# New masks for the last three attention units, a place of its own for the second block's output, and sums inverted in two steps

## The chip, the cores and the metric

The kernel runs on one core of a Trainium2 chip. The metric is the device time of one execution in microseconds (us); the figure for the kernel before is the median of three runs. A profile is one more execution, recorded by the hardware profiler. PE is TensorE (matmul), PEld its weight load, DVE is VectorE, ACT is ScalarE, POOL is GpSimd, SP is SyncE, whose queue issues nearly all DMAs here. All five take their instructions strictly in the order in which the kernel wrote them.

## The reference

A transformer block for 2048 tokens of width 512: attention with 32 heads of 16 in a sliding window of 256, then a SwiGLU feed-forward part of width 1792; both with a modulated layer norm ahead and a gate behind.

```python
mod = (silu(c) @ w_mod).reshape(1, 6, 1, -1)
sa, ca, ga, sb, cb, gb = ...
h = layernorm(x) * (1 + ca) + sa
q, k, v = ...                                  # h @ wqkv, 32 heads of 16
scores = einsum("bhqd,bhkd->bhqk", q, k) * 16 ** -0.5
mask = (i - j >= 0) & (i - j < 256)
o = softmax(where(mask, scores, -1e9)) @ v
x = x + ga * (o @ wo)
h = layernorm(x) * (1 + cb) + sb
out = x + gb * ((silu(h @ w1) * (h @ w3)) @ w2)
```

All of it is float32. Products of weights and activations are made from a high and a low part (float32r), three matmuls for one.

## The kernel before, in words

**Attention.** The 2048 tokens are four blocks b of 512 (`NB`), the 32 heads eight groups g of four (`NQ`); a unit u = 4g + b is one group on one block, 32 units. Three stages run beside each other on different units. `unit_a` projects q and k (L375), ScalarE and GpSimd split them (L381 to L393), and SP puts them into the tile `ring` (L399). `unit_b` makes scores once (L430), takes their maxima on VectorE (L437), turns the maxima (L452) and stores them as more rows of `ring` (L461). `unit_c` makes the scores again, transposed (L681), masks them, takes the exponential, multiplies with the values into `po` (L657), copies `po` (L746) and stores it to DRAM, `o_dr[b]` (L749). The store holds 16 rows of output a head and one row with the sum of its exponentials. Unit 28 to 31 are the last group on the four blocks: after unit 28 the first block is complete in DRAM, after unit 31 the last.

The window's two triangular masks have four forms, chosen per pair of score tiles by a string of eight letters, `MODE` for units 0 to 28 and `MODL` for the last `NL` = 3 units: D adds the mask on VectorE (L689) and ScalarE takes the exponential (L693); E adds it by a second matmul (L684), then L693; P copies the masked squares aside (L716, L718), GpSimd masks them (L726), ScalarE takes their exponential (L730); C merges the two half-empty squares into one (VectorE, L699), takes the exponential of two squares instead of three (L702), and GpSimd cuts the result apart (L709). Where fewer than three squares are left, C becomes D.

**Handover.** Each attention step has a written time in units; those before `TS` = 229.9 are emitted in that order. From there a planner, `Sched.deal`, places all the rest: a list scheduler with an engine's earliest free time, a key for each operation (the smallest key that is ready goes first), a model of DMA transfers and of TensorE's clock, and limits on PSUM banks (`CAPS`). The attention steps left over are `fixed`: they come at their written times (scaled by `KEY` = 1.715 us), the other operations in between. What is emitted is a fixed order for each engine; the keys come from the dictionary `K`.

The other operations: `load_wo` loads the gated output weights (L935) and splits them (L892 on ScalarE, L894 on GpSimd). `load_x1` loads x, 16 tiles (L942). For each block, `o_sums` loads the sums of 32 heads (L952), inverts them (L955) and stores them (L956); `o_part` loads, for each of four parts of eight heads, the output (L971) and its inverses spread over 16 rows (L966), multiplies (VectorE, L982) and splits into a high part (ScalarE, L975) and a low part (VectorE, L978). The loads go to four pairs of staging tiles, (qkr, qk0), (qk1, qk2), (wq00, wq10) and (wq01, wq11), the same for every block; the parts go to the tiles `o0` and `o1`, also the same for every block. `o_proj` multiplies with wo (L998, 48 matmuls a block), adds to x (L1005) and takes the statistics of the second layer norm (L901).

**FFN.** When attention has ended, its memory is closed and `fp_open` makes the FFN's tiles. `load_w` loads the first weights (L1058) and splits them. `ln2(0)` normalizes blocks 0 and 1 (L1109), turns them (L1123), modulates (L1127) and makes the operands (L1140, L1146, L1148); `ffn(half, p)` makes seven products (L1185) twice, gates them (L1208 to L1239), splits (L1255, L1258), and adds the down product (L1276) to x (L1281). Half 0 is blocks 0 and 1, half 1 blocks 2 and 3, with seven steps p each.

Of the kernel before, what the change touches and what calls it, by code (L numbers as in the profile page):

```python
# [8 lines left out]
F32 = mybir.dt.float32  # L9
# [24 lines left out]
MODL = 'DEEPDPDP'  # L34
# [19 lines left out]
CAPS = dict(up=4, dn=2)  # L54
# [6 lines left out]
def dve(n):  # L61
    return 0.067 + 0.00104 * n
# [34 lines left out]
class Sched:  # L97
# [35 lines left out]
    def deal(self):  # L133
# [17 lines left out]
        while left:  # L151
# [21 lines left out]
            if fixed and (best is None or fixed[0][0] <= best[0]):  # L173
                t, fn, e, occ = fixed.pop(0)
# [52 lines left out]

KINDS = dict(scores=("PE", 0.2), top=("DVE", 0.5), parts=("DVE", 0.4), turn=("PE", 0.11), cut=("ACT", 0.16),
# [5 lines left out]
K = dict(wo=0.404, x1=0.976, xb=10.248, opre=-0.989, op=-1.383, o=11.225, l2=2.47, f=35.44,  # L234
         fl=4.282, w=-0.051, dn=0.047, ds=0.032, l3=-43.931)
@with_exitstack
def block_kernel(ctx: ExitStack, tc: tile.TileContext, x, wqk, wv, wo, w13, w2, c, wmod, out):
# [623 lines left out]
    end = (last[-1][0] - TS) * KEY + 1.0  # L861
    fixed = [((t - TS) * KEY, fn, *KINDS[kind]) for t, _, fn, kind in last]
    names = [("st", STB)] * 3 + [("mx", MXB)] * 3 + [("pj", 1)]
    free = [end - 1.0] * 3 + [(8 * (NU - 3) + X["ob"] + 8 + X["tl"] + X["mr"][1] - TS) * KEY + 0.4] * 3 + [0.0]
# [56 lines left out]
    def turn_over():  # L921
# [6 lines left out]
    sch.op("NIL", turn_over, 0.0, 0.0, [], [("x1", t) for t in range(NT)] + [  # L928
        (w, p, k) for w in ("wo", "o") for p in range(2) for k in range(KC)])

    def x1(t):
        return z["x1"][:, t]
# [11 lines left out]
    def o_sums(b, key):  # L944

        v = {}
        src = [("o_dr", b, g) for g in range(NQ)]
        lt = "mT"

        def load():  # L950
            v["lt"] = a1.tile([P, P], F32, name="mT", bufs=2)
            nc.sync.dma_start(v["lt"], o_dr[b].rearrange("(h r) t -> h r t", r=32)[:, DH].rearrange(  # L952
                "h (s t) -> h s t", t=P))
        dma(load, key, src, [lt], 64)
        sch.op("DVE", lambda: nc.vector.reciprocal(v["lt"], v["lt"]), 0.9, key, [lt], [lt])  # L955
        dma(lambda: nc.sync.dma_start(r_dr[b].rearrange("h (s t) -> h s t", t=P), v["lt"]), key, [lt],  # L956
            [("r_dr", b)], 64)

    def o_part(b, k, key):

        v = {}
        on, rn = (("qkr", "qk0"), ("qk1", "qk2"), ("wq00", "wq10"), ("wq01", "wq11"))[k]
# [11 lines left out]
        def hi():  # L974
            nc.scalar.activation(z["o"][0][:, k], v["ot"], AF.Copy)  # L975

        def lo():
            nc.vector.tensor_tensor(out=z["o"][1][:, k], in0=v["ot"],  # L978
                                    in1=z["o"][0][:, k].bitcast(F32), op=ALU.subtract)
        dma(load, key, [("o_dr", b, 2 * k), ("o_dr", b, 2 * k + 1)], [on], 256, occ=0.65, more=1.3)  # L980
        dma(spread, key, [("r_dr", b)], [rn], 256, occ=0.67, more=0.7)
        sch.op("DVE", lambda: nc.vector.tensor_mul(v["ot"], v["ot"], v["rt"]), dve(512) + 0.1, key + 4,  # L982
               [on, rn], [on])
        sch.op("ACT", hi, act(512) + 0.1, key + 4, [on], [("o", 0, k)])
        sch.op("DVE", lo, dve(512) + 0.1, key + 4, [on, ("o", 0, k)], [("o", 1, k)])

    def o_proj(b, key):
# [4 lines left out]
        for i in range(4):  # L992
            bk = Bank("dn")
            t = 4 * b + i
            for k in range(KC):
                def go(i=i, k=k, bk=bk):
                    for n, (h, w) in enumerate(PARTS):
                        nc.tensor.matmul(ps(bk), z["o"][h][:, k, i * P:(i + 1) * P],  # L998
                                         z["wo"][w][:, k], start=(k == 0 and n == 0),
                                         stop=(k == KC - 1 and n == 2))  # L1000
                sch.op("PE", go, 3 * MM[512], key + 2.7 * i + 0.6 * k,
                       [y for kk in (range(KC) if k == 0 else (k,)) for y in
                        (("o", 0, kk), ("o", 1, kk), ("wo", 0, kk), ("wo", 1, kk))], [bk])
            kk = key + 2.7 * (i + 1)
# [392 lines left out]
```

## Time and profile before

| | |
|---|---|
| time, median of 3 runs | 1088.39 us (1086.97 to 1089.33) |
| profiled execution | 1088.08 us, span 1086.3 us |
| busy, share of the span | PE 92%, PEld 66%, DVE 68%, ACT 50%, POOL 51% |
| mean granted clock of TensorE | 0.962 |
| DMA | 131.67 MB, mean 121 GB/s |
| last stores of attention (L749), units 27 to 31 | issued at 505.68, 521.81, 539.46, 556.98, 570.34 us |
| first matmul of the projection, of the FFN | 552.98 us, 623.15 us |

The profile gives times from the start of the span. The granted clock is the share of full speed that TensorE was allowed; a busy TensorE at 0.5 does half the work. "A <- B" reads: A waited for B. SPq is the queue of SP.

### The profile page before, as it was taken

The page shows a single profiled execution, that of the slowest core. Times are in us where ns is not written, and L with a number is a line of the kernel's source. Part 1 is how long each engine was busy: PE and PEld are TensorE (multiplying, and loading weights), DVE is VectorE, ACT ScalarE, POOL GpSimd, SP SyncE. Part 2 cuts the span into 40 slices and gives each one's busy share as a digit, 9 for nine tenths or more (in the row PEclk, how much of TensorE's full clock was granted, in tenths as well). Part 3 has the DMA queues.
Part 4 walks back from the last instruction along what each step waited for, and adds up shares of the span by engine and source line. Part 5 has one row for each costly group of instructions (what it writes and reads, how often), then busy time and mean ns, then how long its engine had stood idle before and what let it go on. Part 6 is the DMA issues. An engine that isn't in the chain of part 4 may idle for free.

```text
span 1086.3 us, 17117 instructions
## 1 busy us (share of the span) xinstructions
PE 1004.3 (92%) x5420; PEld 721.3 (66%) x5420; DVE 738.3 (68%) x1907; ACT 545.2 (50%) x1229; POOL 558.5 (51%) x705
## 2 busy tenths in 40 slices
PE   5999999999999999899796999999998799999998
PEld 3677665566555656565454778888876588878786
DVE  7685677676767676667457975666666866666755
ACT  2435667667766766667553353333344444333322
POOL 7523555566665656564213466876764454353411
PEclk9999999999999999999678899999999899999999
DMA  7522555545454554545556244544432132212102
GB/s 280 175 50 50 147 119 128 128 110 130 115 157 115 133 111 127 127 117 133 166 180 185 78 165 160 176 143 151 147 125 88 50 115 87 88 57 84 54 20 77
DMA packets 74429, 131.67 MB, mean 121 GB/s; under 512 B 8546, under 2 KB 21346, under 8 KB 74212
## 3 DMA queue, kind: packets, MB, share of 16 engines
q1 hardware_dynamic: 73620, 129.54, 42.1%
q10 hardware_dynamic: 720, 1.05, 0.3%
q8 instruction: 43, 0.70, 0.3%
q14 instruction: 46, 0.38, 0.1%
HBM read 79.96 MB, written 30.41 MB: 102 GB/s over the span
## 4 chain that ended last, share of the span: by engine, by line
PE 53%; DVE 16%; DMA 13%; POOL 9%; issue 4%; ACT 3%; SPq 1%; POOLq 0%; ACTq 0%; DVEq 0%
PE mx L1185 9%; DMA ring<-qk 8%; PE st L1185 7%; PE st L1276 6%; POOL qk L393 5%; PE mx L1276 5%; PE mx L430 5%; PE pj L375 4%; PE po L657 4%; PE st L681 3%; PE st L595 3%; PE pj L1185 3%; DVE qk L1258 3%; POOL pt L709 2%; DVE g L1212 2%
## 5 line engine op out<-in xcount | busy, mean ns | idle before, releaser
L437 DVE CUSTOM_DVE_ANT_0 junk<-mx,mskq 128x384 bf16<-128x384 f32 (+2 forms) x512 | 267.6, 529 | 96.1 <-PE mx L430 93.0
L430 PE MATMUL mx<-ring 96*128 96x384 f32 (+2 forms) x512 | 179.4, 363 | 32.1 <-DMA ring<-qk 23.3
L681 PE MATMUL st<-ring 100*128 100x384 f32 (+2 forms) x512 | 162.5, 363 | 5.7 <-DMA ring<-mT 2.7
L894 POOL TENSOR_TENSOR w<-w,w 128x512 fp32r<-128x512 f32 (+2 forms) x60 | 109.1, 1838 | 106.5 <-ACT w L892 106.5
L430 PEld LDWEIGHTS mx<-ring 96*128 96x128 f32 x512 | 97.0, 194 | 94.4 <-DVE mt L437 40.9
L375 PE MATMUL pj<-hT,wq 128*128 128x512 f32 x384 | 156.6, 423 | 1.2 <-DVE hT L295 1.2
L709 POOL TENSOR_SCALAR_AFFINE_SELECT pt<-pt 128x256 f32<-128x256 f32 x204 | 81.8, 406 | 71.0 <-ACT pt L702 63.8
L681 PEld LDWEIGHTS st<-ring 100*128 100x128 f32 x512 | 101.1, 201 | 20.8 <-issue 5.1
L657 PE MATMUL po<-pt,vS 128*17 128x384 f32 (+2 forms) x1408 | 113.1, 406 | 0.0
L393 POOL TENSOR_TENSOR qk<-qkr,qk 128x512 fp32r<-128x512 f32 x64 | 82.2, 1285 | 40.1 <-ACT qkr L381 37.6
L693 ACT ACTIVATE pt<-st 128x384 f32<-128x384 f32 (+2 forms) x174 | 79.3, 460 | 46.1 <-PE st L684 32.1
L702 ACT ACTIVATE pt<-st 128x256 f32<-128x256 f32 x204 | 77.8, 396 | 46.8 <-DVE st L699 45.9
L375 PEld LDWEIGHTS pj<-hT,wq 128*128 128x128 f32 x384 | 73.4, 193 | 26.6 <-issue 18.5
L699 DVE COPY_PREDICATED st<-later,st 128x128 f32<-128x128 uint8 x204 | 59.8, 293 | 38.9 <-PE st L681 38.8
L1216 DVE TENSOR_TENSOR t<-st,t 128x512 f32<-128x512 f32 x62 | 42.3, 686 | 58.5 <-PE st L1185 50.5
L1185 PE MATMUL st<-b,w 128*128 128x512 f32 x300 | 74.8, 391 | 1.7 <-ACT b L1146 1.1
L1185 PE MATMUL mx<-b,w 128*128 128x512 f32 x276 | 69.4, 391 | 2.8 <-DVE b L1148 2.5
L1228 POOL TENSOR_TENSOR t<-t,t 128x512 f32<-128x512 f32 x28 | 36.8, 1315 | 68.1 <-DVE t L1216 68.0
L726 POOL TENSOR_SCALAR_AFFINE_SELECT sm<-sm 128x256 f32<-128x256 f32 x125 | 48.1, 407 | 41.9 <-ACT sm L716 39.1
L1185 PEld LDWEIGHTS st<-b,w 128*128 128x128 f32 x300 | 56.2, 188 | 14.6 <-ACT b L1146 1.5
L1185 PEld LDWEIGHTS mx<-b,w 128*128 128x128 f32 x276 | 51.7, 188 | 14.5 <-DVE b L1148 2.9
L892 ACT ACTIVATE w<-w 128x512 fp32r<-128x512 f32 (+2 forms) x60 | 46.2, 793 | 29.0 <-DMA w<-wsum 21.8
(190 smaller groups left out, 2021.2 us busy)
## 6 DMA issues: line engine op xcount, KB each, us to landing
ring<-qk SPq DMA_DIRECT2D x192, 128.0 KB
o_dr<-os SPq DMA_DIRECT2D x32, 256.0 KB
w<-wsum SPq DMA_DIRECT2D x16, 512.0 KB
w<-w2g SPq DMA_DIRECT2D x14, 512.0 KB
jb<-in_w SPq DMA_DIRECT2D x24, 256.0 KB
w<-wraw SPq DMA_DIRECT2D x16, 384.0 KB
wraw<-in_w SPq DMA_DIRECT2D x7, 768.0 KB
vS<-in_wmod SPq DMA_DIRECT2D x20, 256.0 KB
```

Source lines behind the costliest of these rows:

```text
L375: nc.tensor.matmul(v["ps"], WQ[g][w][:, n // 3], hTp(i, n // 3, b * BT, BT), start=(n == 0), stop=(n == 3 * KC - 1))
L393: nc.gpsimd.tensor_tensor(out=v[n], in0=v["raw"], in1=v[1].bitcast(F32), op=ALU.subtract)
L430: nc.tensor.matmul(v[i][:, :n], queries(NS, a, gq, 1), keys(NS, hh, a, k0, gq + 1 - k0), start=True, stop=True)
L437: nc.vector.tensor_tensor_reduce(out=junk[:, :n], in0=v[i][:, :n], in1=mskq[:, 3 * P - n:], scale=1.0, scalar=-3e38, op0=ALU.add, op1=ALU. ...
L657: nc.tensor.matmul(po[32 * i:32 * i + DH + 1, qb * P:(qb + nq) * P], vS[:, kb, 4 * g + i], pts[i // 2][:, i % 2, c0:c0 + nq], start=first, ...
L681: nc.tensor.matmul(ps[:, :nq], keys(NM, hh, a, kb, 1), queries(NM, a, kb, nq), start=True, stop=not plus)
L693: nc.scalar.activation(held[u, j, a][:, hh, :nq], v[j, a, hh][:, :nq], AF.Exp, scale=SCALE)
L702: nc.scalar.activation(held[u, j, a][:, hh, :2], v[j, a, hh][:, :2], AF.Exp, scale=SCALE)
L709: nc.gpsimd.affine_select(out=pt[:, :, 2 * m], in_=pt[:, :, 0], **w)
L894: sch.op("POOL", lambda: nc.gpsimd.tensor_tensor(out=lo(), in0=src(), in1=hi().bitcast(F32), op=ALU.subtract), 0.06 + 0.0024 * n, key, [kr ...
L1185: nc.tensor.matmul(ps(bk), WT[s, n][w][:, col], BB[t, k][r], start=start and c == 0, stop=stop and c == 5, skip_group_check=True)
L1276: nc.tensor.matmul(ps(bk), tiles[hk + (h,)][:, i * P:(i + 1) * P], W2[y][:, f], start=(m == 0), stop=(m == 5))
```

## The change

Five things change. (1) `MODL` becomes `CECECECE`: in units 29 to 31, of each two pairs of score tiles one merges and one adds its masks by matmul. (2) The sums of a block's first 24 heads are loaded, inverted and stored by a call of their own, which needs only groups 0 to 5; a second call does the last eight heads. A tile of the projection may begin when `n` parts (2, 3, 2, 3 for the four blocks) are there. For each part a table says whether VectorE or GpSimd multiplies and subtracts. (3) Block 1's parts go to a tile of their own, which lies where the second half of x is loaded later; that half is loaded after block 1's projection. (4) The planner's times for the attention steps are shortened towards the end (`TW`), and operations with negative keys may go ahead of an attention step on the same engine. (5) Nearly all keys of the handover and the spacing of the FFN's keys are new, and down products and projections may hold five PSUM banks instead of two.

```diff
-MODL = 'DEEPDPDP'
+MODL = 'CECECECE'
...
-CAPS = dict(up=4, dn=2)
+CAPS = dict(up=4, dn=5)
...
             if fixed and (best is None or fixed[0][0] <= best[0]):
+                t, e = max(free[fixed[0][2]], fixed[0][0]), fixed[0][2]
+                first = [o for key, _, o in ready[e] if key < 0 and o.est <= t and all(
+                    b.i is not None for b in o.bank)]
+                if first:
+                    best = max(free[e], first[0].est), first[0]
+                    fixed.insert(0, None)
...
+def us(t):
+    return KEY * (min(t, TW[0]) - TS + TW[2] * max(0.0, min(t, TW[1]) - TW[0]) + TW[3] * max(0.0, t - TW[1]))
+TW = (231.0, 241.0, 0.8, 0.65)
...
-K = dict(wo=0.404, x1=0.976, xb=10.248, opre=-0.989, op=-1.383, o=11.225, l2=2.47, f=35.44,
-         fl=4.282, w=-0.051, dn=0.047, ds=0.032, l3=-43.931)
+K = dict(wo=-0.364, x1=9.766, xb=-1.267, xl=-0.334, os=1.926, ol=(-20.347, 5.502, 75.149, 3.497),
+         pl=(3.073, -3.847, 6.325, 25.724), pe=(9.152, 48.133, 34.637, 55.18), o=(8.455, 9.391,
+         21.339, 6.756), n=(2, 3, 2, 3), w0=-0.681, l2=-0.513, f=1.271, fl=5.079, by=((('POOL',
+         'POOL'), ('POOL', 'DVE'), ('DVE', 'DVE'), ('DVE', 'DVE')), (('DVE', 'DVE'), ('POOL',
+         'DVE'), ('DVE', 'POOL'), ('POOL', 'DVE')), (('DVE', 'POOL'), ('POOL', 'POOL'), ('DVE',
+         'POOL'), ('DVE', 'POOL')), (('POOL', 'POOL'), ('POOL', 'DVE'), ('DVE', 'DVE'), ('POOL',
+         'POOL'))), w=4.043, dn=0.374, ds=0.12, l3=-12.416)
...
-        z["x1"] = xp.tile([P, NT, D], F32, name="x1")
+        z["x", 0] = xp.tile([P, NT // 2, D], F32, name="x1a")
...
+        o = xp.tile([P, 2 * KC, BT], F32R, name="x1b", bufs=1)
+        z["p"] = [o[:, KC * n:KC * n + KC] for n in range(2)]
...
+    def open_x1(key):
+        def go():
+            z["x", 1] = pools["xp"].tile([P, NT // 2, D], F32, name="x1b", bufs=1)
...
-    def o_sums(b, key):
+    def o_sums(b, g0, g1, key):
...
-        sch.op("DVE", lambda: nc.vector.tensor_mul(v["ot"], v["ot"], v["rt"]), dve(512) + 0.1, key + 4,
-               [on, rn], [on])
+        by, minus = K["by"][b][k]
+        sch.op(by, lambda: on_eng(by).tensor_tensor(out=v["ot"], in0=v["ot"], in1=v["rt"], op=ALU.mult),
+               SPAN[by], key + 0.4, [on, rn], [on])
...
-                       [y for kk in (range(KC) if k == 0 else (k,)) for y in
-                        (("o", 0, kk), ("o", 1, kk), ("wo", 0, kk), ("wo", 1, kk))], [bk])
+                       [y for kk in (range(K["n"][b]) if k == 0 else (k,)) for y in
+                        ((o_of(b), 0, kk), (o_of(b), 1, kk), ("wo", 0, kk), ("wo", 1, kk))], [bk])
...
+        add_(0.2, lambda b=b, ks=ks: o_sums(b, 0, 6, ks), ("os", b))
+        add_(kb, lambda b=b: o_sums(b, 6, 8, K["ol"][b]), ("os", b))
...
+        if b == 1:
+            add_(kb + 0.7, lambda kb=kb: open_x1(kb), "x1")
+            for t in range(NT // 2, NT):
+                add_(kb + 0.8, lambda t=t, kb=kb: load_x1(t, kb + K["xl"] + K["xb"] * (t // 4 - 2) + 0.7 * (t % 4)),
+                     "x1")
...
-    add_(te + 0.75, lambda: load_w(0, 0, te + 1), "w")
-    add_(te + 0.8, lambda: ln2(0, te + K["l2"]), ("ln2", 0))
+    add_(te + 0.75, lambda: load_w(0, 0, K["w0"]), "w")
+    add_(te + 0.8, lambda: ln2(0, K["l2"]), ("ln2", 0))
```

More of the change, by code (lines that the diff above doesn't have):

```diff
@@ L974, in hi @@
         def hi():
[L975 removed]
+            nc.scalar.activation(z[on_][0][:, k], v["ot"], AF.Copy)
         def lo():
[L978 to L979 removed]
+            on_eng(minus).tensor_tensor(out=z[on_][1][:, k], in0=v["ot"],
+                                    in1=z[on_][0][:, k].bitcast(F32), op=ALU.subtract)
         dma(load, key, [("o_dr", b, 2 * k), ("o_dr", b, 2 * k + 1)], [on], 256, occ=0.65, more=1.3)
[L981 to L985 removed]
+        dma(spread, key, [("r_dr", b, 2 * k), ("r_dr", b, 2 * k + 1)], [rn], 256, occ=0.67, more=0.7)
+        by, minus = K["by"][b][k]
+        sch.op(by, lambda: on_eng(by).tensor_tensor(out=v["ot"], in0=v["ot"], in1=v["rt"], op=ALU.mult),
+               SPAN[by], key + 0.4, [on, rn], [on])
+        sch.op("ACT", hi, act(512) + 0.1, key + 0.4, [on], [(on_, 0, k)])
+        sch.op(minus, lo, SPAN[minus], key + 0.4, [on, (on_, 0, k)], [(on_, 1, k)])
     def o_proj(b, key):
@@ L1112, in ln2 @@
                 sch.op("DVE", go, 0.5, key + 3 * t + 0.1 * i,
[L1113 removed]
+                       [("x1", 4 * b + i), "rsB%d" % b, ("mvB%d" % b, i)] + (
+                           [("wqr", m) for m in range(NB)] if xnames[y] == "wqr" else []), [xnames[y]])
         def rows_k(k, key):
```

73 lines of the change are left out of this document (45 added, 28 removed).

## The prediction

> **What bounds the kernel now.** I read the page first, slice by slice (40 slices of 27.2 us), TensorE's busy share and its granted clock.
>
> ```profile
> PE   5999999999999999899796999999998799999998
> ...
> PEclk9999999999999999999678899999999899999999
> ```
>
> TensorE is full at full clock nearly everywhere. Busy share and clock both fall in the 20th to 23rd slice (516 to 625 us), where attention ends, the output projection is made and the feed-forward part (FFN) starts, and, less, in the 32nd, where the FFN changes halves. That is the stretch the diff edits. I then asked for busy time by window there; the columns are PE, PEld, DVE, ACT, POOL (us busy, instructions), clock, DMA share, GB/s.
>
> ```profile
> 513.60:527.20 13.60, 9.09 (x49) 5.19 (x53) 4.95 (x19) 6.01 (x16) 4.64 (x6) 0.59 0.70 179
> 527.20:537.40 10.20, 8.68 (x49) 4.58 (x45) 8.09 (x30) 7.85 (x21) 2.82 (x5) 0.83 0.42 123
> 537.40:557.80 20.40, 18.30 (x88) 8.37 (x86) 8.16 (x15) 13.20 (x36) 2.29 (x6) 0.52 0.71 225
> 557.80:581.60 23.80, 23.80 (x140) 17.39 (x140) 15.09 (x28) 8.01 (x21) 3.78 (x6) 1.00 0.53 164
> 581.60:605.40 23.80, 13.40 (x37) 8.83 (x36) 21.03 (x28) 7.22 (x11) 12.11 (x7) 0.64 0.57 154
> 605.40:622.40 17.00, 16.36 (x87) 13.62 (x86) 16.61 (x29) 8.47 (x14) 5.75 (x5) 1.00 0.21 64
> 622.40:639.40 17.00, 14.00 (x52) 10.41 (x51) 16.69 (x27) 10.63 (x17) 5.61 (x6) 0.90 0.36 119
> ```
>
> Loss of a window is its length less busy time times clock: in order from 513.6 it is 8.2, 3.0, 10.9, 0.0, 15.2, 0.6 and 4.4 us, 42.3 in all. TensorE's work there at full clock is 125.8 - 42.3 = 83.5 us. So the change can win at most about 42 us, and the question for each edit is which of these seven losses it reaches. To see what makes them I read the longest pieces of the chain of waits in 505 to 640 us (start, length, what), then who waited for whom (total, times, longest).
>
> ```profile
> 511.98 5.77 DMA ring<-qk
> 521.81 4.79 DMA o_dr<-os
> 537.64 4.81 DMA ring<-mT
> ...
> 578.53 11.87 DMA w<-wraw
> ...
> 602.28 9.21 DMA qk<-r_dr
> ```
>
> ```profile
> SPq L971 <- DVE o L978: 12.4, 4, 9.8
> ...
> SPq L971 <- DMA o_dr<-os: 3.9, 1, 3.9
> ...
> PE mx L998 <- ACT o L975: 8.1, 1, 8.1
> ...
> PE st L681 <- DMA ring<-mT: 2.7, 2, 1.5
> ```
>
> The first loss (513.6) is ring<-qk, 5.77 us on its way. The third (537.4) is almost all clock: TensorE is busy 18.3 of 20.4 us at 0.52, so the last units run at half speed, bound by TensorE itself. The fifth (581.6) is an empty TensorE, 8.1 us for the split of block 2's first part, which waited for loads that travelled with the first weights (11.87 us), and then half clock. In the last three windows VectorE is busy 54.3 of 57.8 us: it is the second limit there.
>
> **The change part by part.** (1) Masks of units 29 to 31. Per unit the old list has three pairs that add on VectorE (6 L689), two that add by TensorE, three that go to the side (6 L716, 6 L718, 3 L730, 6 L726); the new one has four that merge (8 L699, 8 L702, 8 L709) and four that add by TensorE (unit 31's short tiles add on VectorE instead of merging). Behind the count stand busy us and mean ns.
>
> ```profile
> L689 DVE TENSOR_TENSOR st<-st,mskk 128x256 f32<-128x256 f32 x14 | 5.9, 429 | 7.6 <-PE st L681 7.6
> L699 DVE COPY_PREDICATED st<-later,st 128x128 f32<-128x128 uint8 x5 | 1.5, 293 | 0.0
> L693 ACT ACTIVATE pt<-st 128x384 f32<-128x384 f32 x28 | 13.4, 496 | 10.6 <-DVE st L689 8.3 <-PE st L684 2.2
> L716 ACT ACTIVATE sm<-st 128x256 f32<-128x256 f32 x18 | 7.1, 392 | 1.5 <-PE st L681 1.5
> L718 ACT ACTIVATE pt<-st 128x128 f32<-128x128 f32 x20 | 5.8, 292 | 0.0
> L730 ACT ACTIVATE pt<-sm 128x512 f32<-128x512 f32 x9 | 5.7, 636 | 0.0
> L702 ACT ACTIVATE pt<-st 128x256 f32<-128x256 f32 x5 | 1.9, 410 | 0.4 <-DVE st L699 0.3
> L726 POOL TENSOR_SCALAR_AFFINE_SELECT sm<-sm 128x256 f32<-128x256 f32 x20 | 7.7, 408 | 29.2 <-ACT sm L716 29.1
> L709 POOL TENSOR_SCALAR_AFFINE_SELECT pt<-pt 128x256 f32<-128x256 f32 x6 | 2.4, 405 | 4.4 <-ACT pt L702 4.2
> ```
>
> ScalarE per unit: old 10 x 0.496 + 6 x (0.392 + 0.292) + 3 x 0.636 = 11.0, new 8 x 0.496 + 8 x 0.410 = 7.2, so 3.8 less. VectorE: 2.6 to 2.3. GpSimd: 2.4 to 3.2. TensorE: 4 more mask matmuls a unit, 12 in all; the piece of the chain below is one at half clock, so 0.12 at full: 1.4 us dearer, 2.9 if the clock stays low.
>
> ```profile
> 519.36 0.24 PE st L684
> ```
>
> What this opens: from 527.2 to 557.8 ScalarE was busy 7.85 + 13.20 = 21.1 us, while TensorE's work at full clock was 7.2 + 9.5 = 16.7; so ScalarE would be the limit once the clock is full. With 3.8 us a unit less it no longer is.
>
> (2) Early sums and parts. Today nothing of block 0 is multiplied before its last unit is stored, read back, inverted and spread (the 4.79 us of o_dr<-os and after), and its projection starts at 552.98, though wo was split by 530.2. New: 24 heads of each block are inverted from data stored long ago, and a tile's chain starts with 2 or 3 of 4 parts.
>
> ```profile
> 528.90 1.29 POOL L894 TENSOR_TENSOR wo<-wo,wo 128x512 fp32r<-128x512 f32 x1 [3.00 <-ACT wo L892]
> ...
> 552.98 1.63 PE L998 MATMUL pj<-wo,o 128*128 128x512 f32 x3
> ...
> 577.88 5.61 PE L998 MATMUL st<-wo,o 128*128 128x512 f32 x24
> ```
>
> A block's projection is 48 matmuls of 5.61 / 24 = 0.23: 11.2 us at full clock. The window at 557.8 shows what such filler does: clock 1.00 for 23.8 us. If it comes 12 us earlier (541, halfway between the 530 that data allows and 553), 12 us at half clock become full: 6 us; the shorter ScalarE work ends some of the 2.1 us of idle too. I take 8 of the 13.9 us lost between 527.2 and 557.8; the bounds are 0 (part 4 of a block still hangs on its last unit) and 12.
>
> Cost of it: four reciprocals more, eight small DMAs more, and 16 of 32 multiplies and subtractions go to GpSimd.
>
> ```profile
> L955 DVE RECIPROCAL mT<-mT 128x128 f32<-128x128 f32 x4 | 3.8, 947 | 4.3 <-DMA mT<-o_dr 4.3
> ...
> 561.91 0.54 SPq L952 DMA_DIRECT2D mT<-o_dr  x1
> ...
> 566.71 0.33 SPq L956 DMA_DIRECT2D r_dr<-mT  x1
> ...
> L978 DVE TENSOR_TENSOR o<-wq,o x8: 674/688/2848, 545.2 to 615.5; 128x512 fp32r<-128x512 f32 x8
> ...
> L894 POOL TENSOR_TENSOR wo<-wo,wo 128x512 fp32r<-128x512 f32 x4 | 5.1, 1277 | 10.7 <-ACT wo L892 10.7
> ```
>
> VectorE: 4 x 0.95 more, 16 x 0.69 fewer: 7.2 us less, of value where it is full (581.6 on). GpSimd: 16 x 1.28 = 20.4 us more, beside 37 busy of 125.8; cover enough. SP: 4 x (0.54 + 0.33) = 3.5 us of queue. Behind them in that queue stand the rows of the last maxima (L461) and the stores (L749); TensorE waits for both.
>
> The row of L978 (least, median, most) also shows a price: a subtraction takes 0.69 us, but 2.85 at most. The Trainium skill ("SBUF — State Buffer", section "Who interferes with whom") says that a VectorE instruction with two SBUF inputs and a GpSimd instruction that reads SBUF block each other whole. The trace agrees, by that maximum; by the rule alone the 16 operations moved to GpSimd could hold VectorE for 20.4 us, where the sum here has it relieved.
>
> (3) Block 1 in its own place, second half of x loaded after it. Blocks 1 and 2 no longer wait for the projection of the block before to release its operands. But the staging tiles (qkr, qk1, wq00, wq01 and their partners) are still one set for all blocks, so loads still wait for the subtraction of the block before, as L971 does now (9.8 us). Eight loads of 256 KB, 2.1 MB, move from under attention to after block 1's projection: at the 225 GB/s of the window at 537.4 that is 9.3 us of DMA, now next to the weights. Block 2 needs them only at its additions, after its matmuls, so I cost it at nothing; without that cover 9.3 us.
>
> (4) Weights first, projections ahead of FFN products. In the window at 581.6 (15.2 lost) block 2's first three parts would be made already, and filler would be there while the last part travels; that part now queues behind weights. I take 8 of 15.2, bounds 0 and 13. The last two windows (5.0) are VectorE's; 7 us less there, part of it spent on the shorter stretch: I take 1, bounds -3 and 4.
>
> The first loss (8.2) stays: wo, 1 MB, keeps the smallest key on SP, just ahead of the ring<-qk of the last unit.
>
> ```profile
> 506.45 0.33 SPq L935 DMA_DIRECT2D wo<-wog  x1
> 507.61 4.96 SPq L399 DMA_DIRECT2D ring<-qk  x6
> ```
>
> (5) New spacing of FFN keys and more banks for the down products. From 639.4 on TensorE is full except at the change of halves and at the end.
>
> ```profile
> 800.00:880.00 80.00, 67.92 (x293) 53.42 (x292) 58.57 (x70) 36.15 (x58) 37.98 (x22) 0.94 0.26 89
> ...
> 1065.70:1086.30 20.60, 15.81 (x66) 11.88 (x65) 12.42 (x19) 2.53 (x4) 1.29 (x1) 0.99 0.27 102
> ```
>
> That is 16.2 and 4.9 us lost. Order alone can move some of it either way; I take 0, bounds -4 and 4.
>
> **Sum.** 8 + 8 + 1 - 1.4 = 15.6 us off. The profiled execution took 1088.08 us (span 1086.3, 1.8 around it), 0.3 under the median, 1088.39. So 1072.5, and 1072.8 against the median.
>
> **The rivals.** (a) Slower: an in-order queue stalls inside attention. Block 1's early loads wait for block 0's subtractions on the shared staging tiles; today that wait, 9.8 us, lies at 585, with no attention behind it. Taken up earlier, it stands ahead of the L461 rows of the last unit. Then the attention gain is gone, 9.8 us are added, and of the 9 after it I leave half: 9.8 - 4.5 + 1.4 = 6.7 slower, 1095. It decides from a wait of 5.3 us (2.2 us slower). For it: landing times of 4.8 to 9.2 us in the chain, against a written order that can't adapt; an urgent step now goes ahead of an attention step, so a late DMA holds VectorE's merges as well. Against it: the one wait of such a load inside attention, for o_dr<-os, was 3.9 us. (b) The moved x loads and the weights take what was won after attention: 8 - 1.4 off, less a few us: 1084. For it: DMA share 0.71 at 537.4; against: 0.57 and 0.21 later. (c) GpSimd blocks VectorE for the whole of its ten operations in blocks 2 and 3: 12.8 us against 6.9 saved, 5.9 more on a full VectorE, and only attention's gain left: 1088.1 - 8 + 1.4 + 5.9 = 1087.4. For it: the maximum above; against it: the median stayed at 0.69. It is what the rule of the Trainium skill cited above would do here. (d) The change not doing what it says: the planner could place the early sums late; that is (b) or no change.
>
> **How the numbers follow.** Forecast 0.58, (a) 0.30, (b) 0.06, (c) 0.06. A measurement here tells 0.2%, 2.2 us. (b) is faster; (c) is the same (0.04) or slower (0.02). Faster 0.64, same 0.04, slower 0.32. Low end: 12 + 13 + 4 + 4 - 1.4 = 31.6 would be 1057; I take 1058. High end 1097, a little over (a), leaving out about a third of it. The forecast alone: 1062 to 1083.
>
> **What would show it.** Right: the last store of attention by about 560 instead of 570; clock at 1.00 before 545; the first L998 before 545 and no gap over 4 us near 583; FFN dense by about 615. Attention wrong: SP waiting over 5 us ahead of an L461, or clock at 0.5 through the last two units. After it wrong: VectorE rows of L978 or L982 over 1.5 us in numbers, or L1005 waiting for x. Unit 31's store later than 570 would make the whole forecast wrong.

## The result, and the profile after

The changed kernel took 1104.87 us (median of four runs, 1097.62 to 1105.91), the kernel before 1088.86 us beside it (1086.97 to 1091.91): ratio 1.0109, 95% interval 1.0073 to 1.0145. By that ratio, which is the measure used from here on, it is slower by about 12 us (the plain medians lie 16.0 us apart), where 15.6 us were forecast to be won. The profiled execution took 1105.39 us, its span is 1103.7 us, 17.4 us longer than before. From here on line numbers are those of the changed kernel: scores L456 and L707, values L683, store L775, sums L995/L999/L1000, loads of a part L1021 and L1016, multiply L1033, high part L1025, low part L1028, projection L1049, its addition L1056, layer norm L1160, its turn L1175, operands L1192/L1198/L1200, weights L1109 and their split L918/L920, FFN products L1237, down products L1328.

First the slices of the page of the changed kernel, TensorE's busy share and its granted clock.

```profile
PE   5999999999999999998886789999999799999997
...
PEclk9999999999999999998887898999999899999999
```

The dip is now long rather than deep: the clock's 6 of slice 20 and 7 of slice 21 are gone, but 8s and a 7 run from the 19th slice to the 25th, where before they ended with the 23rd. The windows of the prediction, then five more (PE, PEld, DVE, ACT, POOL busy us and instructions, granted clock, DMA share, GB/s), of the changed kernel:

```profile
513.60:527.20 13.60, 10.41 (x55) 4.96 (x55) 6.26 (x27) 6.92 (x16) 5.10 (x9) 0.67 0.58 174
527.20:537.40 10.20, 7.49 (x44) 4.25 (x42) 8.47 (x26) 4.38 (x11) 5.92 (x8) 0.83 0.75 203
537.40:557.80 20.40, 20.24 (x155) 10.41 (x154) 11.12 (x23) 14.23 (x37) 7.70 (x13) 0.89 0.46 138
557.80:581.60 23.80, 18.04 (x72) 13.43 (x70) 15.09 (x24) 6.60 (x9) 11.29 (x8) 0.86 0.64 201
581.60:605.40 23.80, 15.84 (x55) 11.89 (x55) 18.61 (x21) 4.89 (x8) 13.47 (x9) 0.74 0.52 180
605.40:622.40 17.00, 11.48 (x55) 9.22 (x55) 14.22 (x17) 11.04 (x19) 10.83 (x7) 0.90 0.13 43
622.40:639.40 17.00, 15.80 (x54) 12.22 (x55) 15.67 (x21) 8.52 (x14) 7.33 (x5) 0.75 0.20 69
639.40:680.00 40.60, 35.46 (x142) 28.17 (x141) 26.21 (x32) 11.36 (x17) 27.11 (x22) 0.92 0.39 134
680.00:800.00 120.00, 117.44 (x504) 94.02 (x503) 78.50 (x91) 43.64 (x69) 78.22 (x80) 1.00 0.46 154
800.00:880.00 80.00, 69.76 (x299) 55.13 (x298) 56.86 (x67) 34.63 (x53) 45.37 (x29) 0.96 0.28 93
880.00:900.00 20.00, 17.67 (x76) 14.30 (x77) 12.43 (x18) 10.10 (x17) 8.12 (x6) 1.00 0.36 121
1083.10:1103.70 20.60, 14.52 (x60) 10.59 (x58) 13.11 (x18) 2.88 (x5) 3.53 (x3) 1.00 0.27 102
```

The same view of the kernel before, for the two stretches that the prediction called full:

```profile
639.40:680.00 40.60, 40.53 (x175) 32.91 (x176) 21.80 (x31) 16.34 (x27) 31.86 (x28) 1.00 0.50 168
680.00:800.00 120.00, 120.00 (x521) 97.46 (x520) 75.48 (x96) 47.41 (x74) 88.81 (x85) 1.00 0.47 158
```

Loss is again length less busy time times clock. In us, before and after:

| window | before | after |
|---|---|---|
| 513.6 | 8.2 | 6.6 |
| 527.2 and 537.4 | 13.9 | 6.4 |
| 557.8 | 0.0 | 8.3 |
| 581.6 | 15.2 | 12.1 |
| 605.4 and 622.4 | 5.0 | 11.8 |
| 639.4 | 0.1 | 8.0 |
| 680 | 0.0 | 2.6 |
| 800 to 900 | 16.3 | 15.3 |
| last 20.6 | 4.9 | 6.1 |
| all | 63.6 | 77.2 |

The attention stretch won 7.5 us, nearly the 8 forecast. Behind it, from 557.8 to 800, 20.3 us of loss became 42.8: 28.1 us of empty TensorE and 14.7 us of lowered clock. (Of the 16.3, 0.1 lies behind 880, the change of halves; it ran past 880 in the changed kernel.) All rows together are 13.6 us dearer; the stretches that the table leaves out lost 1.1 us less than before. What remains of the 17.4, some 5 us, is TensorE work by this reckoning, with 1.4 estimated for the masks; the granted clock is given to two digits only, and the 5 us are not broken down further. Who TensorE waited for from 545 to 665 us (total, times, longest), changed kernel:

```profile
PE pj L1175 <- DVE e L1160: 4.5, 3, 2.0
PE pj L1049 <- DVE o L1028: 4.2, 1, 4.2
PE mx L1237 <- ACT t L1271: 3.8, 1, 3.8
PE st L1237 <- ACT b L1198: 3.5, 1, 3.5
PE st L1175 <- DVE g L1160: 3.4, 4, 1.1
PE mx L1237 <- DVE b L1200: 2.0, 1, 2.0
PE pj L1175 <- DVE wqr L1160: 1.6, 1, 1.6
PE mx L1237 <- POOL wo L920: 1.4, 1, 1.4
PE st L1237 <- DVE b L1200: 1.2, 1, 1.2
```

No single wait is as long as the 8.1 us of before; there are nine kinds of short ones. In windows of 4 us the granted clock is 0.50 behind each cluster of them, from 564, 584, 624 and 664 us. Three places make the list, seen in the order of events (timeline: start, length, in brackets the idle time before and what ended it).

*559 us.* SP, VectorE and TensorE, and last the piece of the chain of waits (start, length) that is the store's way to DRAM:

```profile
550.53 0.34 SPq L775 DMA_DIRECT2D o_dr<-os  x1
559.45 0.69 SPq L995 DMA_DIRECT2D mT<-o_dr  x1
...
561.44 0.94 DVE L999 RECIPROCAL mT<-mT 32x128 f32<-32x128 f32 x1 [4.63 <-DMA mT<-o_dr]
562.31 0.62 DVE L1028 TENSOR_TENSOR o<-wq,o 128x512 fp32r<-128x512 f32 x1
...
562.98 0.80 PE L1049 MATMUL pj<-wo,o 128*128 128x512 f32 x1 [4.17 <-DVE o L1028]
...
550.53 8.90 DMA o_dr<-os
```

Block 2's store, issued at 550.53, is what the load of its sums waits for; SP stands 8.5 us at L995, and VectorE stands 4.63 us at the reciprocal, with block 0's last subtraction right behind it in VectorE's order. The subtraction needs nothing of block 2. TensorE waits for it, and the last values of unit 31 stand behind that in TensorE's order.

*578 to 604 us.* The eight normalizations of blocks 0 and 1 beside GpSimd's work, changed kernel:

```profile
578.80 2.59 DVE L1160 TENSOR_SCALAR wqr<-x1a,mvB,rsB 128x512 f32<-128x512 f32 x1 [1.26 <-POOL rsB L939]
581.31 5.91 DVE L1160 TENSOR_SCALAR e<-x1a,mvB,rsB 128x512 f32<-128x512 f32 x3
597.86 5.72 DVE L1160 TENSOR_SCALAR g<-x1a,mvB,rsB 128x512 f32<-128x512 f32 x4 [0.91 <-POOL rsB L939]
...
578.73 6.80 POOL L920 TENSOR_TENSOR w<-w,w 128x1024 fp32r<-128x1024 f32 x3
597.80 1.28 POOL L920 TENSOR_TENSOR w<-w,w 128x512 fp32r<-128x512 f32 x1
599.05 1.44 POOL L1028 TENSOR_TENSOR o<-wq,o 128x512 fp32r<-128x512 f32 x1
600.45 1.44 POOL L920 TENSOR_TENSOR w<-w,w 128x512 fp32r<-128x512 f32 x1
601.85 1.44 POOL L1033 TENSOR_TENSOR qkr<-qkr,qk 128x512 f32<-128x512 f32 x1
```

Each normalization takes 1.5 to 2.6 us here and ends about when a GpSimd operation ends; the turns (L1175) come one by one behind them.

*637 to 665 us.* The projection of block 3 comes last and holds the tiles into which the second step's weights are loaded. TensorE:

```profile
645.59 2.89 PE L1049 MATMUL pj<-wo,o 128*128 128x512 f32 x12
...
656.91 1.44 PE L1237 MATMUL mx<-b,wo 128*128 128x512 f32 x5 [1.37 <-POOL wo L920]
662.11 2.93 PE L1237 MATMUL mx<-b,wo 128*128 128x512 f32 x6 [3.76 <-ACT t L1271]
```

Before, that projection ended at 632.4; here at 648.5, with 6.8 us of other products between it and the first use of the new weights (655.15), where 18 us lay between them before (650.50).

### The profile page after: what moved, and what is told of

Read it like the earlier page. It is cut to its first block, busy times and chain, and to the rows that moved or that the text cites. A ratio compares the mean times of both kernels' runs of the same rounds, so it can differ in the third digit from the quotient of the medians.

```text
span 1103.7 us, 17078 instructions
## 1 busy us (share of the span) xinstructions
PE 1009.3 (91%) x5432; PEld 725.7 (66%) x5432; DVE 752.2 (68%) x1901; ACT 541.4 (49%) x1204; POOL 587.5 (53%) x725
## 4 chain that ended last, share of the span: by engine, by line
PE 43%; POOL 16%; DMA 14%; DVE 12%; issue 9%; ACT 3%; SPq 2%; POOLq 0%; DVEq 0%; ACTq 0%
DMA ring<-qk 7%; PE mx L1237 6%; PE st L1237 5%; PE mx L456 4%; POOL qk L419 4%; PE pj L401 4%; PE st L1328 4%; PE po L683 3%; PE st L707 3%; PE mx L1328 3%; PE st L621 3%; PE pj L1237 2%; POOL w L920 2%; POOL e L834 2%; POOL pt L735 2%
## 5 line engine op out<-in xcount | busy, mean ns | idle before, releaser
L456 PE MATMUL mx<-ring 96*128 96x384 f32 (+2 forms) x512 | 179.6, 364 | 30.4 <-DMA ring<-qk 18.7
L707 PE MATMUL st<-ring 100*128 100x384 f32 (+2 forms) x512 | 160.2, 358 | 3.2 <-ACT pt L728 2.0
L456 PEld LDWEIGHTS mx<-ring 96*128 96x128 f32 x512 | 96.5, 194 | 93.9 <-DVE mt L463 42.2
L920 POOL TENSOR_TENSOR w<-w,w 128x512 fp32r<-128x512 f32 (+2 forms) x60 | 115.9, 1946 | 60.4 <-ACT w L918 48.3
L735 POOL TENSOR_SCALAR_AFFINE_SELECT pt<-pt 128x256 f32<-128x256 f32 x224 | 90.4, 408 | 87.3 <-ACT pt L728 79.4
L728 ACT ACTIVATE pt<-st 128x256 f32<-128x256 f32 x224 | 85.3, 395 | 58.0 <-DVE st L725 57.0
L683 PE MATMUL po<-pt,vS 128*17 128x384 f32 (+2 forms) x1408 | 110.8, 400 | 0.0
L707 PEld LDWEIGHTS st<-ring 100*128 100x128 f32 x512 | 99.3, 197 | 15.8 <-ACT pt L728 5.4
L725 DVE COPY_PREDICATED st<-later,st 128x128 f32<-128x128 uint8 x224 | 65.4, 293 | 47.9 <-PE st L707 47.7
L1237 PE MATMUL st<-b,w 128*128 128x512 f32 x288 | 73.0, 394 | 7.8 <-ACT b L1198 3.5
L1260 ACT ACTIVATE g<-t 128x512 f32<-128x512 f32 x42 | 26.5, 630 | 109.2 <-POOL t L1280 79.5
L1237 PE MATMUL mx<-b,w 128*128 128x512 f32 x306 | 77.7, 396 | 2.0 <-DVE b L1200 2.0
L1237 PEld LDWEIGHTS mx<-b,w 128*128 128x128 f32 x306 | 58.5, 192 | 15.3 <-DVE b L1200 2.4
L1237 PEld LDWEIGHTS st<-b,w 128*128 128x128 f32 x288 | 54.2, 189 | 21.1 <-ACT b L1198 4.0
L918 ACT ACTIVATE w<-w 128x512 fp32r<-128x512 f32 (+2 forms) x60 | 46.4, 796 | 20.9 <-DMA w<-w2g 9.4
L1268 DVE TENSOR_TENSOR t<-st,t 128x512 f32<-128x512 f32 x48 | 32.8, 686 | 34.1 <-PE st L1237 31.7
```

The lines of the kernel that those rows point to most:

```text
L456: nc.tensor.matmul(v[i][:, :n], queries(NS, a, gq, 1), keys(NS, hh, a, k0, gq + 1 - k0), start=True, stop=True)
L683: nc.tensor.matmul(po[32 * i:32 * i + DH + 1, qb * P:(qb + nq) * P], vS[:, kb, 4 * g + i], pts[i // 2][:, i % 2, c0:c0 + nq], start=first, ...
L707: nc.tensor.matmul(ps[:, :nq], keys(NM, hh, a, kb, 1), queries(NM, a, kb, nq), start=True, stop=not plus)
L728: nc.scalar.activation(held[u, j, a][:, hh, :2], v[j, a, hh][:, :2], AF.Exp, scale=SCALE)
L735: nc.gpsimd.affine_select(out=pt[:, :, 2 * m], in_=pt[:, :, 0], **w)
L920: sch.op("POOL", lambda: nc.gpsimd.tensor_tensor(out=lo(), in0=src(), in1=hi().bitcast(F32), op=ALU.subtract), 0.06 + 0.0024 * n, key, [kr ...
```

## The experiments

The letters of the theories are those of the expectations below: in the third experiment C is the spacing of the FFN's keys, in the last three C is chance. A change of a key or of a price makes the planner write a new order for everything behind `TS`, so each such kernel tests its edit and draws a new order at once; where only the engine an operation is emitted on is changed, the order stays. Ratios are to the kernel before, run beside.

**Which part of the change.** Only the masks, in the kernel before:

```diff
-MODL = 'DEEPDPDP'
+MODL = 'CECECECE'
```

> The kernel before with the new masks of units 29 to 31 alone (MODL), all else as it was. Theory 1 (the loss comes after attention, from steps in a fixed order that meet late transfers; the masks are a gain): the last store of attention by 566 us instead of 570, and a time of 1080 to 1086. Rival (the masks themselves cost, through 12 more mask matmuls and GpSimd cutting): 1090 or more, last store after 571.

1.0002 (0.9980 to 1.0024), with the last store at 568.76: neither theory. ScalarE's 3.8 us a unit and the 12 matmuls together come to nothing that can be seen in the time; the interval is 2.4 us either way. Inside attention the masks did something, at least in the one execution that was profiled. The window at 537.4, where the kernel before had a clock of 0.52 and lost 10.9 us:

```profile
537.40:557.80 20.40, 15.93 (x124) 7.80 (x125) 9.63 (x23) 11.61 (x31) 5.73 (x11) 0.92 0.73 232
```

That is 5.7 us of loss, although the projection starts at 552.0, only 1 us earlier than in the kernel before. The next three are the changed kernel with one thing altered: the conversion of the attention steps' times nearer to the measured ones,

```diff
-TW = (231.0, 241.0, 0.8, 0.65)
+TW = (231.0, 243.0, 1.3, 0.8)
```

> The changed kernel with the planner's times of the attention steps stretched to what the trace of the changed kernel shows (TW 231, 243, 1.3, 0.8: the end is planned at 51.5 us instead of 36.6). Theory A (the compressed times are the cause: every other step is written in an order that fits an attention 14 us shorter than it is): the empty stretches near 558 and 580 shrink and the time falls to 1088 or below. Rival B (GpSimd's or the FFN's new order is the cause): 1098 to 1106, unchanged.

1.0048 (1.0021 to 1.0075): a part at most. The losses at 557.8 and 581.6 did shrink, from 20.4 us together to 8.8, but those at 605.4 and 622.4 grew from 11.8 to 15.3. Then the FFN's keys and banks as before,

```diff
-CAPS = dict(up=4, dn=5)
+CAPS = dict(up=4, dn=2)
...
-fl=5.079 ... w=4.043, dn=0.374, ds=0.12, l3=-12.416
+fl=4.282 ... w=-0.051, dn=0.047, ds=0.032, l3=-43.931
```

> The changed kernel with the FFN's spacing, the limit on banks and the key of the second norm as before (fl, w, dn, ds, l3, CAPS). Theory C (TensorE waits at 655 to 669 because the second step's products stand ahead of the first step's down products while their weights still travel, and some 3 us are lost later in the same way): the waits near 655 go and the time falls by 6 to 12, to 1093 to 1098. Rival A (the handover before 650 sets it): under 3 us of change.

1.0098 (1.0059 to 1.0137): no part of it that can be seen; and all 32 multiplications and subtractions on VectorE, for the planner and on the chip,

```diff
-        by, minus = K["by"][b][k]
+        by, minus = "DVE", "DVE"
```

> The changed kernel with all multiplies and subtractions of the parts on VectorE, none on GpSimd. Theory B (GpSimd's 16 operations hold VectorE and the weight splits): the normalizations of 1.4 to 2.6 us fall towards 0.5 to 1, and the time falls by 6 or more, to 1098 or less. Rival A (the order against late transfers): no gain, 1100 to 1110, since VectorE takes 11 us more.

0.9947 (0.9924 to 0.9969). This is the whole difference and more: the change without GpSimd's 16 operations is faster than before.

**The engine or the order.** The fourth experiment altered two things, the engine and the order planned for it. Emitting alone tells them apart: the changed kernel's order with all 16 on VectorE; the fourth experiment's order with the 16 on GpSimd; and the order of before with the same 16 on GpSimd.

```diff
-        return nc.vector if e == "DVE" else nc.gpsimd
+        return nc.vector
```

> The changed kernel with its order on every engine kept; only the 16 operations of the parts that it gives to GpSimd run on VectorE, in their places in the order. Theory B (GpSimd as an engine is the cause: a slower operation that also holds VectorE): 1084 to 1092, near the kernel with all on VectorE and its own order. Rival A' (the order that the planner made for a kernel with GpSimd is the cause, and the engine is not): 1100 to 1106, as the changed kernel.

> The order that the planner made with all parts on VectorE (which ran 0.5% faster than the kernel before), with the 16 operations on GpSimd as in the changed kernel, in their places in that order. Theory B: 1095 or more, at least 8 us above that kernel. Rival A' (order): within 4 us of it, 1083 to 1091.

> The kernel before, its order on every engine kept, with the same 16 of the 32 multiplies and subtractions of the parts on GpSimd. Theory B: slower by 4 us or more, most of it between 581 and 640, where VectorE is full and GpSimd splits the first weights. Rival (GpSimd relieves a full VectorE there): equal or up to 5 us faster.

| order planned for | 16 operations on VectorE | on GpSimd |
|---|---|---|
| the division (changed kernel) | 1.0079 (1.0051 to 1.0107) | 1.0109 (1.0073 to 1.0145) |
| VectorE alone | 0.9947 (0.9924 to 0.9969) | 0.9983 (0.9953 to 1.0014) |
| before | 1 | 1.0018 (0.9995 to 1.0042) |

Along each row the engine costs 0.2% to 0.4%, 2 to 4 us, none of the three beyond its interval by itself but all on one side. Down the first column the order costs 1.3%, 14 us. The fourth and the fifth experiment have the same operations on the same engines; only their order, and the PSUM banks that go with it, differ. So most of the loss is in the written order. How full TensorE is goes with it: 60 to 160 us after the store of unit 28 in the kernel before, the changed kernel, the fourth, the fifth and the sixth experiment (PE instructions are the x behind its busy time):

```profile
581.81:681.81 100.00, 85.89 (x355) 67.04 (x354) 77.73 (x115) 43.35 (x68) 56.78 (x45) 0.90 0.44 138
```

```profile
580.13:680.13 100.00, 78.87 (x301) 61.76 (x302) 76.19 (x91) 35.95 (x56) 60.27 (x44) 0.85 0.34 119
```

```profile
581.34:681.34 100.00, 91.40 (x392) 72.38 (x391) 74.56 (x108) 41.42 (x65) 55.00 (x51) 0.96 0.47 149
```

```profile
574.95:674.95 100.00, 85.98 (x340) 67.72 (x341) 72.59 (x102) 38.46 (x60) 46.22 (x39) 0.88 0.39 130
```

```profile
578.24:678.24 100.00, 91.06 (x381) 72.31 (x382) 71.07 (x98) 40.08 (x62) 64.08 (x55) 0.93 0.43 143
```

355, 301, 392, 340 and 381 matmuls in the same 100 us. The changed kernel's order is the emptier one on either engine: 340 against 392 on VectorE, 301 against 381 on GpSimd. How the 91 between 301 and 392 divide can't be read from it, since each count belongs to one execution: the fifth's took 1094.51 us, well below its median of 1100.88, so the ratios of the table weigh more than these counts.

**Is it one of the three places?** The planner believes that sums can be loaded 2.6 us after a store; the trace said 8.90 us for block 2. Telling it so, with VectorE alone and with the division:

```diff
-        o.est, o.lat = at_, 2.6
+        o.est, o.lat = at_, (2.6, 2.6, 9.0, 8.0)[b]
```

> The kernel with all parts on VectorE, and in the planner the last outputs of blocks 2 and 3 expected 9.0 and 8.0 us after their store instead of 2.6, as the trace of the changed kernel has them. Theory D (VectorE and SP wait for block 2's last sums with block 0's last subtraction behind, 4.2 us of TensorE and then half clock): another 4 to 8 us faster than with 2.6, 1078 to 1083. Rival (something else is late in that place): within 3 us.

0.9943 (0.9912 to 0.9974): beside the 0.9947 without it, nothing.

> The changed kernel, the division of the 16 operations between VectorE and GpSimd kept; only the planner is told that the last sums of blocks 2 and 3 come 9.0 and 8.0 us after their stores (it believed 2.6 us; the trace shows 8.90 us for block 2). Theory G (the reciprocal of those sums, standing ahead of block 0's last subtraction on VectorE, is what breaks the handover): the 4.17 us wait of the first projection on the subtraction of line 1028 near 559 us goes and with it the half-clock window behind it, 4 to 8 us off, 1097 to 1101 us where the changed kernel gives 1105, ratio 1.003 to 1.007. Theory P (the planner's prices: the order is poor because the 16 operations on GpSimd are written down as costing VectorE nothing): this one wait is a small part, less than 3 us, ratio 1.008 to 1.012.

1.0055 (1.0028 to 1.0083), in theory G's range. But G's reason does not hold. TensorE's two costliest kinds of wait from 545 to 665 us in that kernel (total, times, longest):

```profile
PE pj L1175 <- DVE e L1160: 4.4, 3, 2.0
PE pj L1049 <- DVE t L1268: 4.3, 1, 4.3
```

The 4.2 us at L1028 are gone, and a wait of 4.3 us of the projection for another VectorE instruction is there instead. The window at 557.8, which was to win, lost 11.4 us (TensorE busy for 15.26 of 23.8 at 0.81), where the changed kernel lost 8.3. Then block 3 first:

```diff
-pe=(9.152, 48.133, 34.637, 55.18)
+pe=(9.152, 48.133, 34.637, 20.0)
...
+    for o in ups[4:]:        # feed-forward products, step 0
+        for p in proj:       # block 3's projection
+            o.deps.add(p); o.need += 1; p.users.append(o)
```

> The changed kernel with the planner's key of block 3's first three parts at 20.0 instead of 55.18, and with the feed-forward products from the fifth on made to wait for block 3's projection. Theory E (the projection of block 3, last at 648.3 us, holds the tiles that the second step's weights are loaded into, so that only five products are left as cover and the TensorE falls to half clock between 639 and 680 us, 8.0 us lost there): the loss in the 40 us behind the projection's end falls to under 3 us, 5 to 8 us off in all, ratio 1.003 to 1.006. Theory P: the parts of block 3 come late because VectorE and GpSimd hold each other up in the 25 us before, whatever the keys say; TensorE then waits for the parts instead, the time stays within 3 us, ratio 1.008 to 1.013.

1.0067 (1.0042 to 1.0093), between the two ranges. The projection did end earlier, at 636.1, and the 40 us behind it lost 4.7 us instead of the 8.3 behind the end at 648.5; theory E asked for less than 3. Its wait is still there: that of 3.8 us for L1271 is now one of 3.0 us:

```profile
PE mx L1237 <- ACT t L1271: 3.0, 1, 3.0
```

So two of the three places were tried. The new orders were some 5 us faster than the changed kernel's, by ratios whose intervals touch its own; neither place carries the loss alone, and where a wait went, another of like size came.

A candidate for the best version came with these: VectorE alone, the late sums and the measured conversion.

> A candidate for the best version: the changed kernel with all 16 operations on VectorE, the planner told of the late sums as above and with the measured time conversion of the second experiment. Each of the two was worth something by itself (0.6% the conversion, none to 0.1% the sums, both beside plans of their own). If they add, ratio 0.988 to 0.992, about 1080 us; if plans made for VectorE alone only scatter around their own level, 0.992 to 0.997.

0.9949 (0.9926 to 0.9972): the three do not add.

**Is it the planner's price for GpSimd?** It counts 1.29 us of GpSimd for an operation there, and nothing for VectorE. The price put in:

```diff
+        if by == "POOL":
+            sch.op("DVE", lambda: None, 1.0, key + 0.4, [on], [])
...
+        if minus == "POOL":
+            sch.op("DVE", lambda: None, 1.0, key + 0.4, [(on_, 0, k)], [])
```

> The changed kernel with the same 16 operations on GpSimd, but the planner is told that each of them also takes VectorE 1.0 us (in the trace a VectorE operation of 0.68 us takes 1.7 us beside one of GpSimd); nothing else differs, the planner writes a new order by that price. Theory P (the order is poor since it was planned as if GpSimd's operations cost VectorE nothing): most of the 14 us that separate the new order from the one planned for VectorE alone comes back, 1087 to 1095 us, ratio 0.995 to 1.002, near the 0.9983 of VectorE's order with the operations emitted on GpSimd. The rival (orders differ by chance; the division of the engines is not what made this one poor): the ratio stays at 1.005 to 1.012 as in the other plans made with the division.

0.9974 (0.9946 to 1.0002): just what theory P asked for. Half the price, and, as a control, the whole price on ScalarE (`"ACT"` in place of `"DVE"`):

> As the eleventh experiment (the 16 operations divided as in the changed kernel, the planner told that each one on GpSimd also takes time of VectorE), with 0.5 us in place of 1.0 us. Theory P (the missing price made the order poor): part or all of the 13 us comes back, ratio 0.997 to 1.005. Chance (any plan made with this division scatters about its level of 1.005 to 1.011, the eleventh was a lucky one): 1.005 to 1.012.

> The control: the same 1.0 us for each of the operations on GpSimd, but booked on ScalarE, whose operations the trace does not show slowed beside GpSimd (0.61 to 0.63 us for line 1025 in either case). Theory P: nothing comes back, ratio 1.005 to 1.012 as in the other plans with this division. Chance, or slack of any kind in the plan being what helps: 0.995 to 1.003.

1.0007 (0.9974 to 1.0040) and 0.9984 (0.9954 to 1.0014). The control gives back as much, so theory P's reason falls: a price for what VectorE loses beside GpSimd is not what the order needed. With the time of these entries at zero the planner writes the changed kernel's order unaltered, so it was the booked time that made the new orders. Is it any booked time, then? GpSimd's own time for the 16 operations raised and lowered, and a new order with no time added:

```diff
-    SPAN = dict(DVE=dve(512) + 0.1, POOL=1.29)
+    SPAN = dict(DVE=dve(512) + 0.1, POOL=1.7)      # sixteenth; 0.9 in the seventeenth
...
-    add_(te + 0.75, lambda: load_w(0, 0, K["w0"]), "w")
+    add_(te + 0.75, lambda: load_w(0, 0, te + 1), "w")      # eighteenth
```

> The changed kernel with the planner's time for one of the 16 operations on GpSimd at 1.7 us, which is what the longer ones take in the trace (1.72 us), in place of 1.29 us; nothing is booked on VectorE. Theory S (slack booked for these operations repairs the order, whichever engine it is booked on): ratio 0.996 to 1.002. Theory C (plans of this division scatter between 0.997 and 1.011): anything in that range, as often above 1.004 as below.

> The opposite: 0.9 us in place of 1.29 us, so less time than the operations take. Theory S: no better than the changed kernel's plan and likely worse, ratio 1.007 to 1.016. Theory C: 0.997 to 1.011, as often below 1.004 as above.

> A new plan without any time added: the changed kernel with the key of the first feed-forward weights as it was before (the end of attention plus 1 in place of -0.681), which makes the planner's order differ from the 95th operation on. Theory S: ratio 1.005 to 1.012, as in the five other plans without added time (1.0048 to 1.0109). Theory C: 0.997 to 1.011, as often below 1.004 as above.

1.0035 (1.0008 to 1.0062), 0.9980 (0.9948 to 1.0011), 1.0051 (1.0033 to 1.0070). Less time than the operations take gave a better order than more: theory S falls too. The row of the seventeenth for the 60 to 160 us after unit 28's store:

```profile
577.01:677.01 100.00, 85.97 (x347) 66.66 (x348) 72.95 (x96) 40.01 (x61) 58.73 (x44) 0.90 0.41 134
```

347 matmuls, 46 more than the changed kernel, by an order planned from a wrong number. (Such a count ranks no orders by itself: the thirteenth, at 1.0007, had 306 in its profiled execution of 1097.96 us.) The last one asked whether price, late sums and conversion add:

> The changed kernel's division with the price of 1.0 us on VectorE, the late sums of blocks 2 and 3 and the measured time conversion together: a candidate for the best version that keeps all parts of the change. If the three add: 0.3% below before for the price, 0.5% each for the other two on the unpriced plan, ratio 0.988 to 0.994. If the price has already taken what the other two repair: 0.994 to 0.999.

0.9943 (0.9909 to 0.9977), 1085.17 us: no. But it beats both kernels and keeps every part of the change except the shortened times of (4). The eighth is as fast, 1084.88 us (0.9943), without GpSimd's share.

**What is settled.** Twelve orders were planned with this division of the 16 operations (the changed kernel and the experiments 2, 3, 9, 10, 11, 13 to 18): 0.9943 to 1.0109, on average 1.0029. The changed kernel's is the slowest of the twelve. The three planned for VectorE alone lie at 0.9943 to 0.9949. That the order is the cause of most of the loss is shown (the table above); that GpSimd costs 0.2% to 0.4% is likely from three pairs. That the rest is chance among orders is what is left over after G, E, P and S, and is not itself shown: no property of the plan was found that tells a good order from a bad one ahead of the run. Chance alone also sits badly with one thing: all three orders for VectorE alone lie among the best four of the fifteen, 0.8% below the average of the twelve, and GpSimd's own 0.2% to 0.4% explains only part of that. Whether dividing the operations makes the planner's orders worse, and how, stays open.

## Why the prediction was wrong

**What held.** Step (2), the attention stretch: 7.5 us won of the 8 forecast. Projections do fill the last units (first L1049 at 545.73 instead of 552.98) and the clock of the window at 537.4 went from 0.52 to 0.89. But that the filler raised the clock, the reason given, is not shown: the clock was up before the filler came,

```profile
541.00:542.00 1.00, 1.00 (x8) 0.52 (x4) 0.22 (x1) 0.00 (x0) 1.00 (x1) 0.50 0.69 240
542.00:543.00 1.00, 1.00 (x10) 0.31 (x9) 0.98 (x3) 0.89 (x3) 0.23 (x2) 0.98 0.06 16
```

and the masks alone reached 0.92 in that window without it. So the size was right in part by luck. Of the signs, the last store came at 565.07, half of the way to 560, the first projection 0.7 us after 545, and the clock stood at 0.87 from 541 to 545; no gap near 583 was over 4 us (the longest was 2.00), but the FFN was not dense by 615 (clock 0.75 from 622.4). The signs of a failure behind attention did not come either: of VectorE's multiplications and subtractions one took over 1.5 us (1.78), and yet that is where the loss lies. Step (3): the moved loads of x cost nothing, no L1056 waited for one. Step (1): the masks neither won nor lost time, alone.

**The step that failed** is (4), with the "last two windows" beside it: +8 and +1 forecast from 557.8 to 639.4, where the loss rose by 12.0 us instead: 21 of the 33 us between forecast and profile. In the window at 581.6 the loss fell by 3.1, but the one ahead of it, full before, lost 8.3, and the two behind it lost 6.8 more instead of 1 less. The prediction took "filler would be there" from what the data allow. What counts is what each engine's written order allows: block 0's subtraction was ready and stood behind a reciprocal that was not. It read the wait that would go, 8.1 us, and did not price what a new order of some 1500 planned operations puts in the other places. Which property of the order makes these waits stays open.

**The step that was mis-sized** is (5): order alone was costed at 0 with bounds of 4 us either way, and the loss from 639.4 on rose by 10.7 us, from 21.3 to 32.0. Over the whole kernel order measured 14 us between two orders of the same operations (fifth experiment against the fourth), and orders with the division spread over 1.7%, 18 us. The bounds should have come from the size of the losses an order can move, 42 us in the seven windows, not from the two, 16.2 and 4.9 us, that it was asked of. The FFN's own keys, which step (5) spoke of, were not to blame (1.0098 with those of before).

**"Cover enough" for GpSimd** in step (2) was too kind: 2 to 4 us by three pairs, against rival (c)'s 5.9. These are net of the 11 us of VectorE's own work that the move saves. By the rule of the Trainium skill cited there ("SBUF — State Buffer", section "Who interferes with whom"), 20.4 us could have been held up, an estimate; how much of it was held up and hidden, the runs do not tell.

**Rival (a)** had the sign, and its price, 6.7 us slower, was the nearest of all to the 12 measured. Its mechanism came in part: an in-order queue did stall at the handover, SP for 8.5 us. But it stalled for a store's landing, not for block 0's subtractions, and it held the projection, not attention's rows: all last stores came earlier than before. So it was not (a) that made the kernel slower; its sign came true by luck.

## What to carry to other kernels

A change that rewrites a static order is two changes: the edit, and a new draw of the order. Test the edit by emitting it on the old order, and the order by emitting the old operations on the new one; here that took two runs and moved the blame from the engine to the order. And give a new order a spread in the prediction that comes from the stretch it governs: several orders of the same work, run on the chip, are worth more than one taken on trust.

## What the runs showed of the hardware

A store of 256 KB to DRAM, 4.79 us on its way in the chain of before (unit 28's), took 8.90 us here (unit 30's), issued at 550.53; the load that waits for it was issued at 559.45. A one-input VectorE instruction, the normalization L1160, which takes 0.53 to 0.55 us alone, took 1.5 to 2.6 us beside GpSimd's operations. The rule of the Trainium skill ("SBUF — State Buffer", section "Who interferes with whom") lists such instructions with one input among those that can hold the ports shared with GpSimd in their two-port modes; the trace agrees in the lengthening, with 2.59 us beside a GpSimd piece of 6.80 us for three splits; which port is held it does not show. In the fourth experiment, whose order put the four g normalizations where GpSimd was free, they took 0.54 us each:

```profile
L1160 DVE TENSOR_SCALAR g<-x1a,mvB,rsB x4: 539/540/541, 598.5 to 599.9; 128x512 f32<-128x512 f32 x4
```
